# Halved selection for the first units, cheaper weight conversion and a new order of small steps in a top-k attention and MLP kernel

## The chip, the core and the metric

One core of a Trainium2 chip runs the whole program. Its engines are TensorE (matmuls and transposes), VectorE, ScalarE, GpSimd and SyncE, which issues the DMAs. In the profile they are PE (with PEld for its weight loads), DVE, ACT, POOL and SP. Every engine works through its own instructions strictly in their written order and waits on semaphores for the others. The metric is the device time of one execution in microseconds (us), smaller being better.

## What is computed

```python
scores = scale * np.matmul(q, k.transpose(0, 1, 3, 2))     # 8 batches, 8 heads, 576 x 576, head size 64
kth = np.partition(scores, -top_k, axis=-1)[..., -top_k:-top_k + 1]   # top_k = 32
scores = np.where(scores >= kth, scores, -1000000000.0)
attn = np.exp(scores - np.max(scores, axis=-1, keepdims=True))
attn = attn / (np.sum(attn, axis=-1, keepdims=True) + 1e-09)
x = np.matmul(attn, v)                                     # heads side by side: (8, 576, 512)
mu, var = x.mean(-1), x.var(-1)
xn = (x - mu) / np.sqrt(var + 1e-06) * g_ln
out = x + np.maximum(xn @ w_ch1, 0.0) @ w_ch2              # 512 -> 2048 -> 512
```

q, k, v and g_ln are float32. The two weights come as float64, as pairs of 32-bit words, and the kernel makes float32 of them itself.

## The kernel before

**Units.** The work is cut into units. A unit is one block of 128 query rows for both heads of a pair (two tiles of 128 x 576 scores), or, for the last 64 rows of a batch, a "rest" unit that packs both heads into one tile. Four head pairs and eight batches make 160 units. They are grouped into jobs of one batch, one head pair and some query blocks (L743 to 753): batch 0 has jobs with blocks [0, 1], then [2, 3], then the rest [4]; batch 1 has [0, 1] and [2, 3, 4]; all later ones [0, 1, 4] and [2, 3]. The units of a job form a group, whose attention is multiplied with v at once.

**Steps.** The main loop (L900 to 1023) runs one step n per unit and writes the instructions of all engines in a hand-made order. In step n, unit n is in selection on VectorE (`select`, in four parts 0 to 3), unit n + 1 gets its scores on TensorE (`scores`, evicted from PSUM by ScalarE, L335), unit n - 1 is masked on ScalarE (`mask`, `weigh`), and units n - 2 and n - 3 are transposed, multiplied with v (`values`) and scaled by the reciprocal of their sums (`place`). The first EARLY = 8 units are masked and turned one step sooner.

**Selection.** An unhalved unit takes the 8 largest of 576 values four times (L416) and overwrites them in between (L423). A halved unit first splits its scores into larger and smaller of each pair of columns k and k + 288 (`halve`, L363): hi by VectorE (L376), lo by GpSimd on the bits as integers, a + b - hi (L375, L377). It then merges the 16 largest of lo into hi (L390, L385) and selects from 304 columns (L398). Units 0 to 7 are unhalved, all others halved. `halve(n + 1)` stands in step n behind `select(n, 1)`.

**Weights.** 32 pieces of 128 x 512 weights are converted during steps -1 to 16. `split` takes three activations on ScalarE (L180, L181, L184) and a clamp on GpSimd (L185); a step later `shift` is one operation on VectorE (L188) and `join` two or three on GpSimd (L194, L198 for norm's factor in the first 16 pieces, L199). `batches` (L214) says how many pieces a step splits: four ahead of step 0, then 2 and 1 in turn up to step 7, then 2. The sign of a piece lies in one of four buffers, which its join frees.

**Blocks.** When two or three tiles of 128 rows of x are complete, they become a block for norm and MLP: VectorE takes its statistics (`stats`, L623), TensorE transposes x and multiplies (L667, L680, L697). Its matmuls wait in the list `todo`, from which `fill` puts a few into each gap of TensorE's order. `slot` (L864) sets how many: up to step 17 the estimated difference of VectorE's and TensorE's cost, later an even share that leaves 4 us of work when the next block arrives. The first block is given in step 9, and the group ahead of it is finished within step 8 (`quick`).

**Small steps.** `prepare` makes the bias of the exponential out of m's threshold and top, in two operations: on VectorE up to unit 16, on GpSimd later. From batch 2 on, `move` turns one head of most units by a VectorE transpose (L482) and five DMAs in place of TensorE. The reciprocals are at L932.

Of the kernel before, what the change touches and what calls it, by code (L numbers as in the profile page):

```python
# [10 lines left out]
ALU = mybir.AluOpType  # L11
# [5 lines left out]
TOP_K = 32  # L17
# [12 lines left out]
def kernel(  # L30
# [111 lines left out]
    class Piece:  # L142
# [26 lines left out]
        def split(self):  # L169
            def tmp(name, dt):  # L170
                return hpool.tile([P, DM], dt, tag="h", name=name)

            high = self.raw[:, :, 1].bitcast(FP32)
            self.size = tmp("size", U32)
            self.low = tmp("low", FP32)

            pl, tag = ((opool, "o"), (rpool, "r"))[self.i % 2]
            self.sign = pl.tile([P, DM], FP32, tag=tag, name="sign")
            size_f = self.size[:].bitcast(FP32)
            nc.scalar.activation(size_f, high, AF.Abs)  # L180
            nc.scalar.activation(  # L181
                self.low[:], self.raw[:, :, 0], AF.Copy, bias=2.0, scale=2.0**-51
            )
            nc.scalar.activation(self.sign[:], high, AF.Sign)  # L184
            nc.gpsimd.tensor_scalar(size_f, size_f, HIGH_MAX, HIGH_MIN, ALU.min, ALU.max)  # L185

        def shift(self):
# [4 lines left out]
        def join(self):  # L192
            size = self.size[:]
            nc.gpsimd.tensor_tensor(size, size, self.low[:].bitcast(U32), ALU.add)  # L194
            size = size.bitcast(FP32)
            if self.i < NF:
                gain = gcol[:, self.c : self.c + 1].to_broadcast([P, DM])
                nc.gpsimd.tensor_tensor(size, size, gain, ALU.mult)  # L198
            nc.gpsimd.tensor_tensor(self.dst, size, self.sign[:], ALU.mult)  # L199
            ready[self.i] = now[0]  # L200

# [13 lines left out]
    batches = {}  # L215
    queue = list(pieces)
    for n in range(-1, NF):
        count = 4 if n < 0 else 1 + (n + 1) % 2 if n < NF // 2 else 2
        batches[n], queue = queue[:count], queue[count:]
    assert not queue  # L220

# [86 lines left out]
    class Unit:  # L308
        def __init__(self, job, group, qt):
            self.job, self.group, self.qt = job, group, qt  # L310
            self.rest = qt == J
            self.tiles = [(0, 1)] if self.rest else [(0,), (1,)]

            self.moved = False

            self.halved = False
            self.e = None
            self.weighed = 0

# [43 lines left out]
    def halve(u):  # L363

        nt = len(u.tiles)  # L370
        u.lo = lopool.tile([P, 2, HALF], FP32, tag="lo", name="lo")
        u.hi = hipool.tile([P, 2, HALF + TOP_K // 2], FP32, tag="hi", name="hi")
        a, b = u.sc[:, 0:nt, 0:HALF], u.sc[:, 0:nt, HALF:S]
        lo, hi = u.lo[:, 0:nt], u.hi[:, 0:nt, 0:HALF]
        nc.gpsimd.tensor_tensor(lo.bitcast(I32), a.bitcast(I32), b.bitcast(I32), ALU.add)  # L375
        nc.vector.tensor_tensor(hi, a, b, ALU.max)  # L376
        nc.gpsimd.tensor_tensor(  # L377
            lo.bitcast(I32), lo.bitcast(I32), hi.bitcast(I32), ALU.subtract
        )

    def select_halved(u, i):
# [24 lines left out]
    def select(u, i):  # L406

        if u.halved:
            return select_halved(u, i)
        nt = range(len(u.tiles))  # L410
        if i == 0:
            u.cur = [u.sc[:, t] for t in nt]
            u.wk = {}
        m = small.tile([P, 2, 8], FP32, tag=f"m{i}", name=f"m{i}")
        for t in nt:
            nc.vector.max(m[:, t, :], u.cur[t])  # L416
        if i < TOP_K // 8 - 1:
            for t in nt:
                if i == 0:

                    o = (NF - 4 + 2 * t) * DM
                    u.wk[t] = w2[:].rearrange("p f n -> p (f n)")[:, o : o + S]
                nc.vector.match_replace(u.wk[t], m[:, t, :], u.cur[t], LOWEST)  # L423
                u.cur[t] = u.wk[t]
        if i == 0:
            u.top = m
        u.thr = m

    def prepare(u):

        nt = len(u.tiles)
        u.bias = small.tile([P, 2], FP32, tag="bias", name="bias")
        b = u.bias[:, 0:nt]

        engine = nc.vector if u.i < CONVERTING else nc.gpsimd
        engine.tensor_tensor(b, u.thr[:, 0:nt, 7], u.top[:, 0:nt, 0], ALU.subtract)  # L436
        engine.tensor_scalar(b, b, scale, 0.0, ALU.mult, ALU.add)  # L437

    def mask(u, t):
        if u.e is None:  # L440
# [306 lines left out]
    for b in range(B):  # L747
        parts = [[0, 1], [2, 3], [J]]
        if b:
            parts = [[0, 1], [2, 3]]  # L750
            parts[b < 2].append(J)
        for qts in parts:
            jobs += [Job(b, hp, [qts]) for hp in range(NHP)]
    units = []
# [18 lines left out]

    CONVERTING = max(n for n in batches if batches[n]) + 2
    EARLY = jobs[NHP].first
    for u in units[EARLY:]:
        u.halved = True

    for u in units[jobs[5 * NHP].first :]:
        u.moved = not u.rest and u is not u.group.units[-1]  # L780
# [12 lines left out]
    for j in jobs:  # L793
        if j.hp == NHP - 1:
            b = j.b
            step = j.last + (3 if j.last < EARLY else 4)
            tiles = [(b, qt) for g in j.groups for qt in g.qts if qt < J]
            dsts = [[(out[b, t[1] * P : (t[1] + 1) * P, :], full)] for t in tiles]
            if J in j.groups[0].qts and b % 2:

                step += 1
                tiles.append(("r", b // 2))
# [44 lines left out]
    def dve_cost(n):  # L847
        u, ex = at(n), after(n)[0]
        c = 5.0 if u is None else DVE_REST if u.rest else DVE_UNIT
        if u and u.halved:  # L850
            c *= DVE_HALVED
        return c + DVE_MOVE if ex and ex.moved else c

    def give(n):
# [39 lines left out]
    nc.sync.dma_start(grow[:], g_ln.rearrange("(c p) -> c p", p=P))  # L894
    load(fresh[1], nc.sync, nc.scalar)
    scores(units[0])
    load_gain()
    weights(-1, 0)
    weights(-1, 1)
    for n in range(END):  # L900
# [23 lines left out]
            values(g)  # L924
        if u:
            select(u, 0)
        if moved:
            move(ex)
        for store in sent:
            store()  # L930
        for den in recips.pop(n, []):
            nc.vector.reciprocal(den, den)  # L932
        if n == gives_first:
            for blk, i in rows_of.pop(n):
                blk.stats(i)
# [27 lines left out]
        if not quick:  # L963
            weights(n, 1)
        fill()
# [90 lines left out]
```

## Time and profile before

The time is 1665.68 us, the median of 3 runs (1665.18 to 1667.19). The profiled execution spans 1666.8 us:

| engine | busy us | share | instructions |
|---|---|---|---|
| TensorE | 1574.1 | 94% | 7113 |
| VectorE | 1464.5 | 88% | 4476 |
| ScalarE | 1077.2 | 65% | 2759 |
| GpSimd | 664.0 | 40% | 879 |

The largest groups of instructions: hidden matmuls L680, 550.0 us; output matmuls L697, 546.1; VectorE's L398, 460.7, and L385, 368.0; GpSimd's L375 and L377, 197.7 and 196.8; scores L354, 217.4, and their evictions L335, 199.2.

In the lines of the profile, L12 is line 12 of the kernel, "out<-in" names the tiles, "x4" counts instructions merged into one line, and what stands in square brackets is how long the engine was idle before and who ended that. Matmuls of float32 appear as two records each. An average over the span says little here, since the kernel has different limits at different times: it is read in stretches.

### The profile page before, as it was taken

How to read it: one execution, taken by the hardware profiler on the slowest of the kernel's cores; microseconds unless marked ns; L12 is line 12 of the kernel's file. 1: busy time of each engine (PE TensorE's matmuls, PEld its weight loads, DVE VectorE, ACT ScalarE, POOL GpSimd, SP SyncE). 2: the span in 40 equal slices, each digit the busy share in tenths (PEclk: the TensorE clock that was granted, in tenths of full speed). 3: DMA queues.
4: the chain of work that ended last, by engine and by line, in shares of the span. 5: the costliest groups of instructions: out<-in, count | busy, mean ns of one | idle time of the engine just before them, and what ended most of it. 6: DMA issues, size and time to landing. Idle time of an engine off the chain costs nothing.

```text
span 1666.8 us, 25284 instructions
## 1 busy us (share of the span) xinstructions
PE 1574.1 (94%) x7113; PEld 955.1 (57%) x7113; DVE 1464.5 (88%) x4476; ACT 1077.2 (65%) x2759; POOL 664.0 (40%) x879
## 2 busy tenths in 40 slices
PE   3568989989999999999999999999999999999998
PEld 1346556566555575755547575745547575755564
DVE  5998999999999999999999999899998999998000
ACT  5677967767666776767666675767666676665310
POOL 5567854343433434343343434343243433333010
PEclk9758999999999999999999999999999999999999
DMA  7423333001331133213231233112331132111000
GB/s 176 100 64 108 89 58 59 22 14 27 76 81 51 53 76 81 65 54 69 59 86 51 55 73 83 52 54 70 65 89 44 53 81 74 52 46 47 26 13 13
DMA packets 301203, 104.58 MB, mean 63 GB/s; under 512 B 246276, under 2 KB 283144, under 8 KB 301064
## 3 DMA queue, kind: packets, MB, share of 16 engines
q1 hardware_dynamic: 296328, 102.39, 24.4%
q10 hardware_dynamic: 4736, 0.59, 0.3%
q8 instruction: 57, 0.93, 0.2%
q14 instruction: 82, 0.67, 0.1%
HBM read 74.58 MB, written 28.31 MB: 62 GB/s over the span
## 4 chain that ended last, share of the span: by engine, by line
PE 71%; DVE 21%; issue 4%; ACT 2%; POOL 1%; DMA 1%; ACTq 0%; POOLq 0%; DVEq 0%; SPq 0%
PE hps L680 25%; PE ops L697 24%; PE scps L354 8%; PE av L563 6%; DVE m L398 5%; DVE hi L385 4%; PE tp L505 4%; DVE hi L390 2%; DVE m L416 2%; PE av L570 2%; DVE w L423 2%; DVE lo L385 1%; DVE hi L376 1%; DVE size L188 1%; PE tp L667 1%
## 5 line engine op out<-in xcount | busy, mean ns | idle before, releaser
L680 PE MATMUL hps<-xT,w 128*128 128x256 f32 (+1 forms) x2048 | 550.0, 411 | 2.7 <-ACT xT L672 2.3
L697 PE MATMUL ops<-w,h 128*128 128x512 f32 x1152 | 546.1, 599 | 0.0
L398 DVE MAX8 m<-hi 128x8 f32<-128x304 f32 x1088 | 460.7, 458 | 2.3
L680 PEld LDWEIGHTS hps<-xT,w 128*128 128x128 f32 x2048 | 372.1, 191 | 108.5 <-issue 17.3
L385 DVE MATCH_REPLACE8 hi<-m,hi 128x304 f32<-128x304 f32 x816 | 368.0, 456 | 0.0
L375 POOL TENSOR_TENSOR lo<-sc 128x576 int32<-128x576 int32 (+1 forms) x152 | 197.7, 1301 | 316.3 <-ACT sc L335 156.9
L697 PEld LDWEIGHTS ops<-w,h 128*128 128x128 f32 x1152 | 200.2, 191 | 169.9 <-issue 164.6
L377 POOL TENSOR_TENSOR lo<-lo,hi 128x576 int32<-128x576 int32 (+1 forms) x152 | 196.8, 1295 | 141.9 <-DVE hi L376 139.7
L354 PE MATMUL scps<-kT,qT 64*128 64x288 f32 (+3 forms) x1344 | 217.4, 433 | 32.4 <-DVE qT L304 20.9
L335 ACT COPY sc<-scps 128x288 f32<-128x288 f32 x576 | 199.2, 409 | 62.3 <-PE scps L354 51.0
L442 ACT ACTIVATE e<-sc,m 128x576 f32<-128x576 f32 x288 | 224.3, 779 | 9.7 <-DVE m L398 6.2
L452 ACT ACTIVATE e<-e,bias 128x576 f32<-128x576 f32 x288 | 224.6, 780 | 2.9 <-DVE bias L437 2.5
L390 DVE MAX8 hi<-lo 128x8 f32<-128x288 f32 x544 | 221.8, 443 | 2.6 <-POOL lo L377 1.5
L354 PEld LDWEIGHTS scps<-kT,qT 64*128 64x128 f32 (+1 forms) x1344 | 122.4, 181 | 146.6 <-issue 56.2
L505 PEld LDWEIGHTS tp<-ident,e 128*128 128x128 f32 x864 | 110.9, 147 | 115.9 <-ACT e L452 51.7
L505 PE MATMUL tp<-ident,e 128*128 128x128 f32 x864 | 138.1, 285 | 38.2 <-ACT e L452 37.9
L692 ACT ACTIVATE h<-hps 128x256 f32<-128x256 f32 (+1 forms) x256 | 105.9, 414 | 96.5 <-PE hps L680 93.8
L436 POOL TENSOR_TENSOR bias<-m,m 128x2 f32<-128x2 f32 (+1 forms) x143 | 27.8, 195 | 303.6 <-DVE m L398 303.6
L563 PE MATMUL av<-pt,vb 128*64 128x256 f32 (+2 forms) x1088 | 146.7, 413 | 0.0
L376 DVE TENSOR_TENSOR hi<-sc 128x576 f32<-128x576 f32 (+1 forms) x152 | 138.8, 913 | 5.5 <-ACT sc L335 5.5
L385 DVE MATCH_REPLACE8 lo<-hi,lo 128x288 f32<-128x288 f32 x272 | 118.2, 440 | 0.0
L517 ACT COPY pt<-tp 128x512 f32<-128x512 f32 x128 | 74.6, 583 | 62.1 <-PE tp L505 60.5
(79 smaller groups left out, 1295.0 us busy)
## 6 DMA issues: line engine op xcount, KB each, us to landing
turned<-sc SPq DMA_DIRECT2D x72, 256.0 KB, 2.0
pt<-turned SPq DMA_DIRECT2D x288, 64.0 KB, 2.0
vb<-in_v_dram SPq DMA_DIRECT2D x136, 128.0 KB, 2.5
raw<-in_moe_w_ch_dram SPq DMA_DIRECT2D x32, 512.0 KB, 4.0
kin<-in_k_dram SPq DMA_DIRECT2D x128, 72.0 KB, 2.5
qin<-in_q_dram SPq DMA_DIRECT2D x120, 72.0 KB, 2.5
out_dram<-o SPq DMA_DIRECT2D x32, 256.0 KB, 2.2
ends<-in_v_dram SPq DMA_DIRECT2D x136, 16.0 KB, 2.2
```

Source lines behind the costliest of these rows:

```text
L335: nc.scalar.copy(u.sc[:, t, s * HALF : (s + 1) * HALF], made[s][t][:, 0:HALF])
L354: nc.tensor.matmul(ps[i * R : i * R + ql, o : o + width], qT[r, q0 : q0 + ql], kT[r, k0 : k0 + width], start=True, stop=True,)
L375: nc.gpsimd.tensor_tensor(lo.bitcast(I32), a.bitcast(I32), b.bitcast(I32), ALU.add)
L385: nc.vector.match_replace(x[:, t], m[:, t, :], x[:, t], LOWEST)
L390: nc.vector.max(u.hi[:, t, o : o + 8], u.lo[:, t])
L398: nc.vector.max(m[:, t, :], u.hi[:, t])
L442: nc.scalar.activation(u.e[:, t], u.sc[:, t], AF.Prelu, bias=u.thr[:, t, 7:8], scale=-1.0, alpha=SLOPE)
L452: nc.scalar.activation(u.e[:, t], u.e[:, t], AF.Exp, bias=u.bias[:, t : t + 1], scale=-scale / SLOPE, accum_out=g.den[:, col : col + 1],)
L505: nc.tensor.transpose(ps[:, c * P : (c + 1) * P], u.e[:, t, c * P + t * R : (c + 1) * P + t * R], ident[:],)
L563: nc.tensor.matmul(av[h * D : (h + 1) * D, 0 : g.nq], vb[:, h * J + c, :], g.ptB[:, 0 : g.nq // 32, c, :] if h else g.pt[:, c, 0 : g.nq], ...
L680: nc.tensor.matmul(ps["h"][:, 0:N], w1[:, c, f * P : (f + 1) * P], xT[0][:, c, 0:N], start=(c == 0), stop=(c == NC - 1),)
L697: nc.tensor.matmul(ps[i][:], hT[f][:, i * P : (i + 1) * P], w2[:, f, :], start=(f == 0), stop=(f == NF - 1),)
```

## The change

It has six parts. (1) The first eight units are halved too, with both hi and lo by VectorE; for the others, GpSimd's two operations now both come behind VectorE's, as a - hi + b. (2) Norm's factor is multiplied into the sign by ScalarE in `split`, no longer by GpSimd in `join`. (3) Steps 0 to 7 split two pieces each, and steps 8 to 15 two and one in turn. (4) A bias on VectorE is one operation per tile, with the top as scalar operand, instead of two per unit. (5) Within a step, `move` and the reciprocals come behind the halving and the turn of new heads, and `stats` behind `select(u, 2)` (not in the first block's step). (6) In the last batch the rest units come first, as jobs of their own, and the last two tiles of batch 6 wait to form one block with the rest tile. They are for relieving GpSimd and VectorE at the beginning, for fewer waits in VectorE's order, and for smaller blocks at the end.

```diff
             nc.scalar.activation(self.sign[:], high, AF.Sign)
+            if self.i < NF:
+                nc.scalar.mul(self.sign[:], self.sign[:], gcol[:, self.c : self.c + 1])
             nc.gpsimd.tensor_scalar(size_f, size_f, HIGH_MAX, HIGH_MIN, ALU.min, ALU.max)
...
             size = size.bitcast(FP32)
-            if self.i < NF:
-                gain = gcol[:, self.c : self.c + 1].to_broadcast([P, DM])
-                nc.gpsimd.tensor_tensor(size, size, gain, ALU.mult)
             nc.gpsimd.tensor_tensor(self.dst, size, self.sign[:], ALU.mult)
...
-        count = 4 if n < 0 else 1 + (n + 1) % 2 if n < NF // 2 else 2
+        count = 4 if n < 0 else 2 if n < NF // 2 else 1 + (n + 1) % 2
...
-        nc.gpsimd.tensor_tensor(lo.bitcast(I32), a.bitcast(I32), b.bitcast(I32), ALU.add)
         nc.vector.tensor_tensor(hi, a, b, ALU.max)
+        if u.i < EARLY:
+
+            nc.vector.tensor_tensor(lo, a, b, ALU.min)
+            return
         nc.gpsimd.tensor_tensor(
-            lo.bitcast(I32), lo.bitcast(I32), hi.bitcast(I32), ALU.subtract
+            lo.bitcast(I32), a.bitcast(I32), hi.bitcast(I32), ALU.subtract
         )
+        nc.gpsimd.tensor_tensor(lo.bitcast(I32), lo.bitcast(I32), b.bitcast(I32), ALU.add)
...
-        engine = nc.vector if u.i < CONVERTING else nc.gpsimd
-        engine.tensor_tensor(b, u.thr[:, 0:nt, 7], u.top[:, 0:nt, 0], ALU.subtract)
-        engine.tensor_scalar(b, b, scale, 0.0, ALU.mult, ALU.add)
+        if u.i < CONVERTING:
+
+            for t in range(nt):
+                nc.vector.tensor_scalar(
+                    b[:, t : t + 1], u.thr[:, t, 7:8], u.top[:, t, 0:1], scale,
+                    ALU.subtract, ALU.mult,
+                )
+            return
+        nc.gpsimd.tensor_tensor(b, u.thr[:, 0:nt, 7], u.top[:, 0:nt, 0], ALU.subtract)
+        nc.gpsimd.tensor_scalar(b, b, scale, 0.0, ALU.mult, ALU.add)
...
             parts = [[0, 1], [2, 3]]
-            parts[b < 2].append(J)
+            if b < B - 1:
+                parts[b < 2].append(J)
+            else:
+                parts = [[J]] + parts
...
+            if b == B - 2 and units[-1].job.b == B - 1 and J - 1 in j.groups[0].qts:
+
+                kept = (tiles, dsts)
+                continue
             if J in j.groups[0].qts and b % 2:
+                if not tiles:
+                    tiles, dsts = kept
...
     scores(units[0])
+    halve(units[0])
     load_gain()
...
         if u:
             select(u, 0)
-        if moved:
-            move(ex)
         for store in sent:
             store()
-        for den in recips.pop(n, []):
-            nc.vector.reciprocal(den, den)
...
             select(u, 1)
-        if nxt and nxt.halved:
+        if nxt:
             halve(nxt)
         if n in turns:
             turn_heads(turns[n])
...
-        for blk, i in rows_of.pop(n, []):
-            blk.stats(i)
+        for den in recips.pop(n, []):
+            nc.vector.reciprocal(den, den)
+        if moved:
+            move(ex)
         if not quick:
             weights(n, 1)
...
             select(u, 2)
+        for blk, i in rows_of.pop(n, []):
+            blk.stats(i)
```

More of the change, by code (lines that the diff above doesn't have):

```diff
@@ L314, in __init__ @@
             self.moved = False
-            self.halved = False
             self.e = None
@@ L374, in halve, with select @@
         lo, hi = u.lo[:, 0:nt], u.hi[:, 0:nt, 0:HALF]
-        nc.gpsimd.tensor_tensor(lo.bitcast(I32), a.bitcast(I32), b.bitcast(I32), ALU.add)
         nc.vector.tensor_tensor(hi, a, b, ALU.max)
+        if u.i < EARLY:
+            nc.vector.tensor_tensor(lo, a, b, ALU.min)
+            return
         nc.gpsimd.tensor_tensor(
-            lo.bitcast(I32), lo.bitcast(I32), hi.bitcast(I32), ALU.subtract
+            lo.bitcast(I32), a.bitcast(I32), hi.bitcast(I32), ALU.subtract
         )
-    def select_halved(u, i):
+        nc.gpsimd.tensor_tensor(lo.bitcast(I32), lo.bitcast(I32), b.bitcast(I32), ALU.add)
+    def select(u, i):
         nt = range(len(u.tiles))
@@ L404, in select_halved @@
             u.thr = m
[L406 to L427, printed above, removed]
     def prepare(u):
@@ L775 @@
     EARLY = jobs[NHP].first
-    for u in units[EARLY:]:
-        u.halved = True
     for u in units[jobs[5 * NHP].first :]:
@@ L849, in dve_cost @@
         c = 5.0 if u is None else DVE_REST if u.rest else DVE_UNIT
-        if u and u.halved:
-            c *= DVE_HALVED
+        c *= DVE_HALVED
         return c + DVE_MOVE if ex and ex.moved else c
```

## The prediction

> **What bounds the kernel now.** I read first where each engine is busy, in stretches of 50 us (columns: stretch, then busy us and instruction count for each engine, granted TensorE clock, DMA share, GB/s).
>
> ```profile
> core 0: us, PE busy (x) PEld busy (x) DVE busy (x) ACT busy (x) POOL busy (x), PEclk, DMA share, GB/s
> 0.00:50.00 50.00, 15.83 (x51) 9.13 (x51) 32.37 (x66) 28.61 (x61) 27.32 (x35) 1.00 0.64 147
> 50.00:100.00 50.00, 30.33 (x118) 17.94 (x120) 49.73 (x109) 38.17 (x91) 27.73 (x27) 0.66 0.47 114
> 100.00:150.00 50.00, 37.24 (x155) 26.57 (x154) 45.14 (x121) 31.82 (x76) 32.46 (x29) 0.73 0.22 67
> 150.00:200.00 50.00, 48.50 (x234) 30.23 (x233) 49.66 (x153) 48.24 (x117) 44.18 (x39) 1.00 0.42 117
> 550.00:600.00 50.00, 50.00 (x252) 32.00 (x250) 50.00 (x162) 36.34 (x94) 21.52 (x27) 1.00 0.28 68
> 1600.00:1650.00 50.00, 50.00 (x187) 34.52 (x186) 0.00 (x0) 8.77 (x20) 3.16 (x4) 1.00 0.03 6
> ```
>
> TensorE is full from about 450 us to 1661.8, where its last matmul ends, and VectorE is the full one in the first 150. A busy TensorE need not run at its peak, so I compared every run of equal matmuls (say eight records of L680) with the fastest tenth of its kind: from 450 to 1500 the excess is about 1 us in 50. So after 450 the time is a fixed amount of TensorE work, and nothing that VectorE, ScalarE or GpSimd saves there counts. The excess, gaps included, is 29 us in 150 to 350 and 7 in 350 to 450. What can move the end is (1) when the first block's hidden matmuls start, at 132.3 now, (2) these 36 us, (3) TensorE work added or removed.
>
> Next, what holds TensorE in 150 to 450 (waiter, releaser, total us, times, longest):
>
> ```profile
> PE tp L667 <- POOL x L638: 5.3, 2, 4.8
> PE scps L354 <- DVE qT L304: 4.2, 2, 3.3
> PE tp L505 <- ACT e L452: 3.2, 3, 1.8
> PE scps L354 <- ACT x L579: 2.5, 2, 1.8
> ```
>
> VectorE or its followers end all of these. Third, ScalarE from unit 1's masks to unit 8's (31 to 112 us), its busy time and waits:
>
> ```profile
> 31.00:112.00 81.00, 46.25 (x179) 27.97 (x179) 74.04 (x159) 60.63 (x141) 48.97 (x46) 0.74 0.38 97
> ```
>
> ```profile
> ACT oT L575 <- PE av L570: 9.1, 3, 3.9
> ACT sc L335 <- PE scps L354: 5.3, 8, 1.1
> ```
>
> Of 81.0 us it works 60.6 and waits 14.4 for TensorE. Last, VectorE in order of time:
>
> ```profile
> 38.92 0.82 DVE L188 TENSOR_SCALAR size<-size 128x512 uint32<-128x512 uint32 x1 [6.55 <-POOL size L185]
> ...
> 137.36 1.00 DVE L436 TENSOR_TENSOR bias<-m,m 128x2 f32<-128x2 f32 x1
> ...
> 147.62 2.40 DVE L188 TENSOR_SCALAR size<-size 128x512 uint32<-128x512 uint32 x2
> ```
>
> It waits 6.55 us once for GpSimd's joins. A bias of two columns takes 1.00 and two shifts 2.40 where free ones take 0.16 and 0.75: they wait out a running GpSimd instruction.
>
> **The skill.** The Trainium skill, GPSIMD Engine Reference, section 8 (Key points), says that GpSimd shares its SBUF interfaces with VectorE and contends with instructions of two SBUF inputs or in a 2-port mode. The trace agrees: L376 takes 0.74 us (median of 80) with GpSimd idle at its start and 1.23 (mean of 72) with it busy. VectorE: DVE Perf Modes, The perf-mode tier table, gives fp32 tensor_scalar twice tensor_tensor's rate; here L188 advances 512 columns in 0.335 us and L376 576 in 0.676. Perfetto Trace Analysis, Identifying the Most-Contended Engine, warns that matmul busy share doesn't measure distance from the peak; hence the comparison above.
>
> **Part 1, halves for the first eight units.** Unhalved, a unit costs VectorE 8 x 0.668 (L416) + 6 x (0.065 + 0.659) (L423) = 9.69 us. On halves: max and min 2 x 0.676, 4 x 0.360 (L390), 2 x 0.427, 8 x 0.377 (L398), 6 x 0.443 = 9.3. It saves 0.4 a unit, if min costs what max does and finds GpSimd idle; a GpSimd instruction in the way would add up to 1.3. But unit 1's halving is now queued in step 0 and waits for its scores, whose evictions stand on ScalarE behind the first four pieces (20.93 us now).
>
> **Part 2, norm's factor.** GpSimd loses 16 x 1.04 us (L198). ScalarE gains 16 multiplications. An independent 512-column activation starts 0.56 us after the one before; one that reads its predecessor's result must wait for it to end (L184 takes 0.66), so a piece grows from 1.69 to 2.38.
>
> **Part 3, two pieces a step.** Steps 1, 3, 5, 7 get one more piece each (1.69 on ScalarE), steps 9, 11, 13, 15 one less.
>
> **Parts 1 to 3 together, up to the first block.** ScalarE's first four pieces end 4 x 0.69 = 2.8 later, so unit 1's scores are there at about 25.0, VectorE having finished select(0, 1) at 17.4: a wait of 7.6 us takes the place of the 6.55. Behind it are turn, shifts and the rest of unit 0, and behind the shifts GpSimd's joins, which free the sign buffers. ScalarE's step 1 starts at 34.7 instead of 31.5 (+3.2). From there to step 8 it gets 4 x 1.69 + 10 x 0.69 = 13.7 us more. Its slack is 81.0 - 60.6 - 12.2 = 8.2, because the waits for av (9.1) and most of those for scores recur: av comes behind scores on TensorE, and those wait for ScalarE to free PSUM. So step 8 starts 3.2 + 13.7 - 8.2 = 8.7 us later. Step by step I get 8.3 (119.6 for 111.3): an odd step of 14.5 us, an even one of 11.0, against 23.3 for two now. ScalarE replaces VectorE as the bound there. The chain from step 8 to the first hidden matmul (quick values, x, two pieces, scores, xT) has 1.1 us of idle ScalarE to lose, so the hidden start moves from 132.3 to **139.5: +7.2 us**. It could be +4, if the multiplication overlapped like the rest (0.13 x 16 = 2 us) and scores came sooner, or +9.
>
> **Part 4, from there to unit 17.** VectorE reaches unit 11 4.4 us late (its bias and shifts save 2.8). Units 11 to 15 took 53.7: 43.0 of selection and halving, 4.6 of shifts, 5.5 of biases, 0.6 of rest. Now there are 8 shifts instead of 10, right behind the max and before GpSimd can start its subtraction: 2.7. Whether a one-column tensor_scalar waits for GpSimd no row shows: at least 0.35 each, at most the 1.1 of now, 1.8 to 5.5 for five. With 0.9 of other contention, 48.4 to 52. Unit 16 saves 1 to 2. So unit 17 starts between 3 us earlier and 1 later: I take 1 earlier. TensorE allows it: behind the later start it can recover 3.5 us of its own excess by unit 16 and is still ahead of VectorE, so most of the 6.6 us that it waits at 208 to 218 go.
>
> **Part 5, the order of later steps.** With both GpSimd operations behind the max, L376 no longer waits: 1.2 us between units 17 and 22, 0.4 at 330. At 336.5 TensorE waits 4.8 us for x: statistics move behind select(u, 2), and GpSimd has two operations of 1.4 before it: +1.3. Reciprocals move some 2.3 to 3.7 us back, and ScalarE's scaling of x waits for them with its evictions behind it (1.4, 2.0 and 1.2 us at 296 to 330 now). Scores there are a step ahead of VectorE, which hides it. Moves cost nothing: values that read them come two steps later. After 350 VectorE saves another 2.5 us (L376), which may shorten the 4.8 us that TensorE loses at 444 to 448, where a mask waits for VectorE's m; I count 2.
>
> **Part 6, the last batch's order.** The rest tiles get groups of their own: av costs 2.41 + 0.89 instead of 2.95, four times: +1.4. The second unit of each pair is now last in its group, so TensorE turns its second head instead of a DMA: 4 x 0.44 = +1.8. The same blocks are computed, and TensorE has no gap there to close.
>
> **Sum:** -1 (unit 17) - 1.2 - 0.4 + 1.3 - 2 + 3.2 = -0.1, so **1665.6 us**, no change.
>
> **Rivals.** *Faster:* the early delay is small. If the hidden start moves by 2 only, unit 17 comes some 6 us earlier, and the rest sums to about -8: 1658. For it: 36 us of excess are there to be had, and 20 us of ScalarE's 81 are idle. Against it: 14 of these are waits that recur. *Slower:* the delay stays. If the one-column bias and min wait for GpSimd as now, and ScalarE's later scaling holds TensorE, only about 3 of the 7.2 come back; with +1.3 and +3.2 that is +8: 1673. For it: TensorE is at its peak from 132 to 205 but for 3.5 us, and can't catch up more. Against it: VectorE's waits at 137 to 218 are real and have fewer causes left. A third, that k and q loads for four one-unit jobs in a row arrive late, adds 1 to 3 us at the end and belongs to the slower side; 8 issues take 4 us and land 2.5 later, inside a step of 9.
>
> **Numbers.** Forecast 0.40, faster 0.33, slower 0.27. The range 1656 to 1674 takes in both rivals. The forecast spreads over the bound of 3.3 us on either side, so faster by over 0.2% gets 0.38, within 0.30, slower 0.32.
>
> **What would show it.** A wait of VectorE of 7 to 8 us for sc at about 17; ScalarE's evictions for unit 9 at about 119 instead of 111; the first hidden matmul near 139; L436 gone, and its tensor_scalar near 0.2 or near 1.0; L376 near 0.74 throughout; TensorE's excess in 150 to 450 well under 36. A hidden start before 134, or ScalarE still idle at 50 to 100, would prove the central step wrong.

## The result, and the profile after

The changed kernel takes 1679.47 us (median of 4 runs, 1678.92 to 1683.84); the kernel before takes 1665.54 beside it (4 runs, 1665.18 to 1667.19). The ratio is 1.0087, with a 95% interval of 1.0069 to 1.0106: 14 us slower, where the prediction said 1665.6, no change, and 1674 at most. The profiled execution spans 1682.0 us against 1666.8; it is the slowest of the four, some 4 us above the others, so single microseconds below are taken from several traces.

First, where each engine is busy, in the stretches shown of before:

```profile
core 0: us, PE busy (x) PEld busy (x) DVE busy (x) ACT busy (x) POOL busy (x), PEclk, DMA share, GB/s
0.00:50.00 50.00, 15.03 (x49) 8.20 (x50) 33.17 (x92) 33.85 (x68) 22.42 (x29) 1.00 0.67 168
50.00:100.00 50.00, 31.86 (x102) 16.99 (x101) 42.59 (x141) 39.47 (x86) 24.95 (x24) 0.93 0.45 106
100.00:150.00 50.00, 34.01 (x123) 20.72 (x121) 43.30 (x131) 33.84 (x79) 31.43 (x27) 0.63 0.31 90
150.00:200.00 50.00, 49.28 (x244) 34.80 (x243) 45.70 (x151) 42.28 (x103) 35.60 (x32) 0.97 0.20 59
550.00:600.00 50.00, 50.00 (x230) 29.34 (x229) 49.93 (x166) 36.08 (x89) 21.76 (x31) 1.00 0.28 67
1600.00:1650.00 50.00, 50.00 (x204) 35.16 (x203) 1.64 (x4) 10.93 (x27) 5.16 (x8) 1.00 0.03 11
```

VectorE is no longer full between 50 and 100 (42.6 of 50 us, against 49.7). In the two stretches shown after 550 TensorE is as full as before, so most of the loss lies ahead of them or is more work. The first hidden matmul, in order of time on TensorE, starts at 143.46 us instead of 132.30:

```profile
143.46 8.92 PE L665 MATMUL hps<-xT,w 128*128 128x256 f32 x31 [2.98 <-ACT xT L657]
```

ScalarE from unit 1's masks to unit 8's is now the stretch 35 to 124, 89 us instead of 81. Its busy time, and then what it waits for:

```profile
35.00:124.00 89.00, 56.53 (x179) 30.26 (x179) 75.53 (x251) 73.01 (x161) 47.30 (x45) 0.84 0.40 104
```

```profile
ACT oT L560 <- PE av L555: 12.3, 3, 4.4
ACT sc L332 <- PE scps L351: 2.8, 7, 0.5
```

ScalarE works 73.0 of 89 us and waits 15.1 for TensorE. Its waits for VectorE have gone, which in the kernel before (31 to 112 us) were:

```profile
ACT e L442 <- DVE m L416: 2.7, 1, 2.7
ACT e L452 <- DVE bias L437: 2.5, 3, 0.9
```

So ScalarE is the bound here. Next, VectorE in order of time:

```profile
23.72 0.76 DVE L372 TENSOR_TENSOR hi<-sc 128x576 f32<-128x576 f32 x1 [6.38 <-ACT sc L332]
26.84 3.52 DVE L190 TENSOR_SCALAR size<-size 128x512 uint32<-128x512 uint32 x4
...
133.80 0.33 DVE L416 TENSOR_SCALAR bias<-m,m 128x1 f32<-128x1 f32 x2
```

The wait for unit 1's scores is there, 6.4 us at 17.3. A unit's bias, two operations now, takes 0.33 us. Last, what holds TensorE between 150 and 450, and between 400 and 800 (waiter, releaser, total us, times, longest):

```profile
PE tp L652 <- POOL x L623: 4.6, 1, 4.6
PE tp L490 <- ACT e L437: 3.4, 3, 1.8
PE scps L351 <- DVE den L950: 2.3, 1, 2.3
PE scps L351 <- DVE qT L303: 0.8, 1, 0.8
```

```profile
PE av L548 <- DMA vb<-in_v_dram: 2.4, 2, 1.8
PE scps L351 <- ACT xT L657: 0.9, 1, 0.9
```

Two waits are new: for the reciprocals `den`, and for the DMA that brings v.

**An account of TensorE's time.** As in the prediction, each run of equal matmuls is compared with the fastest tenth of its kind, here over all 18 traces. From the first hidden matmul on, that makes a sum: the start, the excess over the fastest (gaps included), the work at its fastest, and 5 us after the last matmul.

| kernel | hidden start | excess to 350 us | 350 to 800 | after 800 | work | span |
|---|---|---|---|---|---|---|
| before | 132.3 | 30.6 | 14.8 | 16.0 | 1468.1 | 1666.8 |
| changed | 143.5 | 25.5 | 19.7 | 16.8 | 1471.4 | 1682.0 |
| difference | +11.2 | -5.1 | +4.9 | +0.8 | +3.3 | +15.2 |
| predicted | +7.2 | -8.5 | -2 | 0 | +3.2 | -0.1 |

(Predicted, to 350: 8.2 recovered up to unit 17, 1.2 and 0.4 less of L376, 1.3 more for late statistics.) The experiments take these columns one after another.

### The profile page after: what moved, and what is told of

Same layout as the page of the kernel before. It is cut to its first block, busy times and chain, and to the rows that moved or that the text cites. A ratio compares the mean times of both kernels' runs of the same rounds, so it can differ in the third digit from the quotient of the medians.

```text
span 1682.0 us, 25369 instructions
## 1 busy us (share of the span) xinstructions
PE 1589.8 (95%) x7201; PEld 962.7 (57%) x7201; DVE 1423.7 (85%) x4551; ACT 1092.0 (65%) x2783; POOL 644.7 (38%) x863
## 4 chain that ended last, share of the span: by engine, by line
PE 56%; issue 3%; ACT 1%; DMA 0%; DVE 0%; POOL 0%; SPq 0%; POOLq 0%; ACTq 0%
PE hps L665 19%; PE ops L682 19%; PE scps L351 6%; PE av L548 5%; PE tp L490 3%; PE av L555 2%; PE tp L652 1%; PE xo L587 0%; PE tp L523 0%; DMA turned<-sc 0%; POOL o L695 0%; DMA vb<-in_v_dram 0%; ACT sc L332 0%; ACT xT L657 0%; ACT e L427 0%
## 5 line engine op out<-in xcount | busy, mean ns | idle before, releaser
L400 DVE MAX8 m<-hi 128x8 f32<-128x304 f32 x1152 | 487.9, 460 | 3.3
L377 POOL TENSOR_TENSOR lo<-sc,hi 128x576 int32<-128x576 int32 (+1 forms) x152 | 195.9, 1289 | 554.1 <-DVE hi L372 331.1
L387 DVE MATCH_REPLACE8 hi<-m,hi 128x304 f32<-128x304 f32 x864 | 390.1, 457 | 0.0
L351 PE MATMUL scps<-kT,qT 64*128 64x288 f32 (+3 forms) x1344 | 224.0, 433 | 41.5 <-DVE qT L303 21.8
L392 DVE MAX8 hi<-lo 128x8 f32<-128x288 f32 x576 | 235.3, 445 | 16.9 <-POOL lo L380 15.7
L372 DVE TENSOR_TENSOR hi<-sc 128x576 f32<-128x576 f32 (+1 forms) x160 | 113.3, 708 | 118.2 <-ACT sc L332 117.9
L380 POOL TENSOR_TENSOR lo<-lo,sc 128x576 int32<-128x576 int32 (+1 forms) x152 | 194.8, 1281 | 11.9
L548 PE MATMUL av<-pt,vb 128*64 128x256 f32 (+2 forms) x1152 | 152.8, 404 | 2.5 <-DMA vb<-in_v_dram 2.4
L387 DVE MATCH_REPLACE8 lo<-hi,lo 128x288 f32<-128x288 f32 x288 | 125.3, 441 | 0.0
L548 PEld LDWEIGHTS av<-pt,vb 128*64 128x64 f32 x1152 | 78.6, 142 | 70.3 <-issue 29.3
```

The lines of the kernel that those rows point to most:

```text
L351: nc.tensor.matmul(ps[i * R : i * R + ql, o : o + width], qT[r, q0 : q0 + ql], kT[r, k0 : k0 + width], start=True, stop=True,)
L377: nc.gpsimd.tensor_tensor(lo.bitcast(I32), a.bitcast(I32), hi.bitcast(I32), ALU.subtract)
L548: nc.tensor.matmul(av[h * D : (h + 1) * D, 0 : g.nq], vb[:, h * J + c, :], g.ptB[:, 0 : g.nq // 32, c, :] if h else g.pt[:, c, 0 : g.nq], ...
```

## Experiments

"Changed" below is the changed kernel; a time's ratio is always to the kernel before, measured beside it. Four of the experiments (undo_gain, undo_pieces, undo_order and undo_last) were to part three theories: A, ScalarE's load before the first block; B, the last batch's order; C, the new places of move, reciprocals and stats.

**ScalarE's load.** Part 2 or part 3 undone, then both, and both alone on the kernel before. The edits, in the order pieces, factor:

```diff
-        count = 4 if n < 0 else 2 if n < NF // 2 else 1 + (n + 1) % 2
+        count = 4 if n < 0 else 1 + (n + 1) % 2 if n < NF // 2 else 2
...
-            if self.i < NF:
-                nc.scalar.mul(self.sign[:], self.sign[:], gcol[:, self.c : self.c + 1])
...
+            if self.i < NF:
+                gain = gcol[:, self.c : self.c + 1].to_broadcast([P, DM])
+                nc.gpsimd.tensor_tensor(size, size, gain, ALU.mult)
```

> The changed kernel (1679.5 us) with part 2 undone: norm's factor is again multiplied in by GpSimd, not by ScalarE. Theory A (ScalarE is overloaded up to the first block, and the late start of the hidden matmuls, 143.5 us against 132.3, is carried to the end one for one): ScalarE has 14 x 0.7 = 9.8 us less before step 8, of which its step time follows about half, so the hidden start falls to about 138 and the time to about 1674. Theory B (the early delay is hidden later, and the last batch's order costs the time): under 2 us less, 1678. Theory C (the new places of move, reciprocals and stats eat what the later steps could win back): under 2 us less, 1678.

> The changed kernel with part 3 undone: steps 0 to 7 split two and one piece in turn, steps 8 to 15 two. Theory A: ScalarE has 4 x 2.4 = 9.6 us less before step 8, so the hidden start falls to about 137 and the time to about 1673, if the four pieces that now fall in steps 9 to 15 don't hold TensorE there. Theory B: under 2 us less. Theory C: under 2 us less.

> The changed kernel with parts 2 and 3 undone: norm's factor on GpSimd, and two and one pieces in turn up to step 7. Theory A: ScalarE has its old load, steps 1 to 8 take 23.5 us for two again or less, the hidden start falls from about 142 to 131 or 132, and the time by 10 to 11 us to about 1669. If the start and the end aren't tied one for one (undoing part 3 alone brought the start 7 us forward and the end only 3), the time falls by 6 us only, to 1673.

> The kernel before with parts 2 and 3 alone: norm's factor on ScalarE and two pieces in each of steps 0 to 7. Theory A: the hidden start goes from 131 (three traces: 130.1 to 132.3) to about 142, and the end follows as far as TensorE has no stall left to absorb it: by 5 to 7 us, 1671 to 1674, since undoing both in the changed kernel gave back 6.5. If the end follows in full: 1677. If VectorE's late biases and halves had hidden it: under 1668.

| kernel | ratio (95%) | hidden start | excess to 350 | 350 to 800 |
|---|---|---|---|---|
| changed | 1.0087 (1.0069 to 1.0106) | 143.5 | 25.5 | 19.7 |
| undo_gain | 1.0057 (1.0040 to 1.0074) | 137.8 | 25.7 | 20.1 |
| undo_pieces | 1.0068 (1.0053 to 1.0083) | 135.8 | 26.7 | 19.0 |
| undo_gain_pieces | 1.0048 (1.0034 to 1.0061) | 130.1 | 27.8 | 19.9 |
| gain_pieces_alone | 1.0026 (1.0017 to 1.0036) | 139.9 | 25.4 | 14.6 |

The multiplication and the doubled pieces bring the late start: either is worth some 5 to 8 us of it, both about 12 in the changed kernel. Theory A holds in its first half. The end doesn't follow one for one: of the 12 us that undoing both brings forward, 0.39% of the time, 6.5 us, comes out at the end, and on the kernel before the two add 4.4 us, not 8.6. TensorE's excess is smaller behind a later start (25.4 against 30.6 up to 350). VectorE is less far behind: in gain_pieces_alone it starts unit 17 3.8 us later (219.8 against 216.0, the mean of four traces of the old order), where the hidden start is 8.6 later, so its results are ready sooner after TensorE wants them. The intervals of undo_gain and undo_pieces overlap both that of changed and that of undo_gain_pieces, so the times don't settle what either does alone.

Why was the start so late? Here is ScalarE in order of time between the last pt copy and the copy of oT, in a step with two pieces of the kernel before and then of the changed one:

```profile
74.81 0.29 ACT L539 COPY pt<-tp 128x128 f32<-128x128 f32 x1
76.19 0.40 ACT L335 COPY sc<-scps 128x288 f32<-128x288 f32 x1 [1.09 <-PE scps L354]
77.15 1.00 ACT L335 COPY sc<-scps 128x288 f32<-128x288 f32 x3 [0.56 <-PE scps L354]
80.94 0.37 ACT L575 COPY oT<-av 128x256 f32<-128x256 f32 x1 [2.79 <-PE av L570]
```

```profile
82.93 0.27 ACT L524 COPY pt<-tp 128x128 f32<-128x128 f32 x1
83.08 1.01 ACT L332 COPY sc<-scps 128x288 f32<-128x288 f32 x3
84.44 0.40 ACT L332 COPY sc<-scps 128x288 f32<-128x288 f32 x1 [0.34 <-PE scps L351]
89.20 0.37 ACT L560 COPY oT<-av 128x256 f32<-128x256 f32 x1 [4.36 <-PE av L555]
```

From the last pt to oT it is 6.13 us before and 6.27 after: av needs the last pt, and ScalarE needs av. What it no longer waits for scores it waits for av: 4.44 us of waits in this stretch became 4.70. None of this took up the added work.

**The order within a step.** All of part 5 undone, then the place of `move` alone undone; then, on the kernel before, move late; move late but with the k and q loads behind it; and move late with v's loads ahead of the k and q loads and of move. The edit of undo_move, from behind the loads to behind select(u, 0); late_move is the same the other way:

```diff
+        if moved:
+            move(ex)
...
         if n in turns:
             turn_heads(turns[n])
...
                 load(fresh[later], nc.sync, nc.sync)
...
-        if moved:
-            move(ex)
```

> The changed kernel with part 5 undone: move and the reciprocals directly behind select(u, 0), stats ahead of the weights, as before. Theory C: the stalls of TensorE at 281 (2.5 us), 341 (4.7) and 451 to 456 (6.7) shrink or go, and the time falls by 5 us or more, to 1674. Theories A and B: within 2 us of 1679.5; the stall at 341 shrinks by 1.3 us at most.

> The changed kernel with one piece of part 5 undone: move stands directly behind select(u, 0) again, ahead of the turn of new heads and the eight k and q loads; reciprocals and stats stay where the change put them. Theory D (the move's six DMAs now stand on SyncE's queue behind the eight loads of a step with a turn, and the loads of v behind them, so av waits for v at 456 and 675 us): the waits for vb go, TensorE's excess in 400 to 800 falls from 15 us to about 10, and the time falls by 4 to 6 us, to about 1674, as with all of part 5 undone. Theory C' (reciprocals or stats are what costs): no change, 1679.

> The kernel before with one edit: move stands behind the turn of new heads and the loads of k and q, as in the changed kernel. Theory D: v lands late in the steps with a turn, the excess in 400 to 800 rises by 4 to 5 us, and the time from 1665.7 to about 1670. Theory C': no change, 1665.7. The prediction counted nothing for this edit.

The loads put behind move, as an edit of late_move:

```diff
         if n in turns:
             turn_heads(turns[n])
-            later = fresh.index(turns[n]) + 1
-            if later < len(fresh):
-                load(fresh[later], nc.sync, nc.sync)
         if moved:
             move(ex)
+        if n in turns:
+            later = fresh.index(turns[n]) + 1
+            if later < len(fresh):
+                load(fresh[later], nc.sync, nc.sync)
```

> The kernel before, with move behind the turn of new heads as in late_move (1.0029 of before), but with the loads of k and q put behind move, so that SyncE issues the move's transfers ahead of them. On VectorE the order is that of late_move. Theory D (it is the order on SyncE's queue that costs): as before, 1665.7, excess in 400 to 800 at 10. If move's place on VectorE is what costs: as late_move, 1670.5.

Then, from late_move again, v's loads taken from the end of the step to ahead of the turn of new heads:

```diff
+        if n > EARLY and mk and mk is units[mk.job.last]:
+            load_values(mk.job)
         if n in turns:
             turn_heads(turns[n])
...
-        for x in (u if n < EARLY else None, mk if n > EARLY else None):
-            if x and x is units[x.job.last]:
-                load_values(x.job)
+        if n < EARLY and u and u is units[u.job.last]:
+            load_values(u.job)
```

> The kernel of late_move (1.0029 of before; move behind the turn of new heads and the k and q loads) with the loads of v issued ahead of all of these in their step. Theory D' (v lands late because its loads are last on SyncE's queue, behind a move that becomes ready later): no wait for vb, excess in 400 to 800 back at 10, 1665.7 as before. If move's place on VectorE costs: 1670.5.

| kernel | ratio (95%) | hidden start | excess to 350 | 350 to 800 |
|---|---|---|---|---|
| undo_order | 1.0044 (1.0029 to 1.0059) | 141.2 | 21.7 | 14.9 |
| undo_move | 1.0052 (1.0039 to 1.0065) | 142.0 | 22.2 | 17.3 |
| late_move | 1.0029 (1.0019 to 1.0040) | 131.1 | 30.6 | 19.5 |
| move_then_load | 1.0056 (1.0044 to 1.0069) | 130.1 | 30.5 | 21.7 |
| late_move_early_v | 0.9996 (0.9988 to 1.0004) | 131.8 | 30.5 | 14.7 |

Moving one VectorE operation and its five DMA issues makes the kernel before 0.29% slower, 4.8 us, nearly all of it as excess between 350 and 800 (3.1 us at 430 to 455 us, 0.5 at 639 and 1.2 at 667, the last two within av). SyncE's DMA issues of a step with a turn of new heads show how. Before, and then changed:

```profile
436.49 0.34 SPq L487 DMA_DIRECT2D turned<-sc  x1
438.51 1.75 SPq L489 DMA_DIRECT2D pt<-turned  x4
440.36 2.00 SPq L278 DMA_DIRECT2D kin<-in_k_dram  x4
442.47 2.17 SPq L278 DMA_DIRECT2D qin<-in_q_dram  x4
444.69 0.49 SPq L290 DMA_DIRECT2D vb<-in_v_dram  x1
```

```profile
444.84 1.94 SPq L277 DMA_DIRECT2D kin<-in_k_dram  x4
446.88 2.06 SPq L277 DMA_DIRECT2D qin<-in_q_dram  x4
449.04 0.44 SPq L472 DMA_DIRECT2D turned<-sc  x1
451.61 1.90 SPq L474 DMA_DIRECT2D pt<-turned  x4
453.56 0.43 SPq L289 DMA_DIRECT2D vb<-in_v_dram  x1
```

SyncE issues in order and waits in between: L474 comes only when L472's transfer has landed, 2.0 to 2.6 us after its issue. In the changed kernel, from 400 to 800 us, SyncE's own waits for this are:

```profile
SPq L474 <- DMA turned<-sc: 43.4, 22, 3.9
```

(The Trainium skill, DMA: Bandwidth & Descriptors, Rules for kernel authors, asks for exactly this wait where one DMA reads what another wrote; this is its price for all that stands behind.) v stands last: it is issued 8.7 us after the first k load instead of 4.3, and in the changed kernel av waits for it:

```profile
456.08 5.58 PE L548 MATMUL av<-pt,vb 128*64 128x320 f32 x16 [1.78 <-DMA vb<-in_v_dram]
```

My first explanation, that the eight loads ahead of move are the harm, fell with move_then_load: with move ahead of them it got slower still (1.0056 against 1.0029). The trace shows the wait that grew there:

```profile
PE av L563 <- DMA vb<-in_v_dram: 4.5, 2, 3.0
```

What counts is how long v stands behind a move that becomes ready late. In late_move the k and q issues at least fill the time until move is ready; in move_then_load they, and v behind them, wait for move and its landing (k is issued at 442.07 instead of 438.27 us). late_move_early_v decides that v is what is late: move is as late on VectorE and its issue as late as in late_move (443.06 against 442.47 us), only v goes first,

```profile
436.05 0.43 SPq L290 DMA_DIRECT2D vb<-in_v_dram  x1
...
443.06 0.43 SPq L487 DMA_DIRECT2D turned<-sc  x1
```

and the loss is gone. (In late_move the waits list names ScalarE's score copies for 1.6 us of av's wait and v's DMA for 0.5 only. Where several semaphores are waited for, one name is shown; the edit, not that name, is the evidence. Another wait that late_move brings, 1.8 us for `e` from ScalarE at about 435 us, stays at 1.3 with early v, and yet the excess from 430 to 455 is 4.6 us there against 4.8 of before; so it isn't the loss.)

Undo_move is not all of part 5: its excess from 350 to 800 is 17.3 against 14.9 with the whole order undone. From halves_bias_old_order below, stats alone were put late:

```diff
-        for blk, i in rows_of.pop(n, []):
-            blk.stats(i)
         if not quick:
             weights(n, 1)
...
             select(u, 2)
+        for blk, i in rows_of.pop(n, []):
+            blk.stats(i)
```

> The kernel of halves_bias_old_order with stats alone behind select(u, 2), as in the changed kernel. If stats make the wait of 2.3 us for the rest tile at 450: as halves_bias, 1665.5. If the reciprocals do: as halves_bias_old_order, 1662 to 1664.

It takes 0.9990 (0.9981 to 0.9998) against 0.9971 (0.9959 to 0.9982) with stats early: 3 us, though the two intervals just touch. In the two profiles 2.4 us of it show as excess. On TensorE, in order of time, this wait is new:

```profile
450.14 0.66 PE L653 MATMUL tp<-ident,r 128*128 128x128 f32 x4 [1.95 <-POOL r L624]
```

It counts for 0.7 us of the excess only (15.6 against 14.9 from 350 to 800), because TensorE waits less just ahead of it. The other 1.6 us lie before 350, nearly all at 338 us, where the same eight matmuls take longer behind a wait that both kernels have. In late_stats, and then in halves_bias_old_order:

```profile
338.62 5.76 PE L683 MATMUL ops<-w,h 128*128 128x512 f32 x8
```

```profile
336.18 4.22 PE L683 MATMUL ops<-w,h 128*128 128x512 f32 x8
```

These eight take 4.2 to 5.8 us in the other traces too, with early stats as with late ones (5.48 in pool_order_alone, with early ones). So the times show that late stats cost something, and the wait at 450 shows one place; how much of the 3 us belongs to it stays open.

With the reciprocals late as well (halves_bias) it is 0.9993: the reciprocals cost nothing that these runs can tell.

**The last batch's order.** Part 6 undone:

```diff
-            if b < B - 1:
-                parts[b < 2].append(J)
-            else:
-                parts = [[J]] + parts
+            parts[b < 2].append(J)
...
-            if b == B - 2 and units[-1].job.b == B - 1 and J - 1 in j.groups[0].qts:
-
-                kept = (tiles, dsts)
-                continue
             if J in j.groups[0].qts and b % 2:
-                if not tiles:
-                    tiles, dsts = kept
```

> The changed kernel with part 6 undone: the last batch's rest units are back in the first jobs, the last blocks are as before. Theory B (the order of the last batch costs what the unit times seem to show, 8 us): 1671.5. Theory A and C: it costs what the prediction counted, 4 x 0.35 of av and 4 x 0.44 of transposes: 1676.3.

The ratio is 1.0051 (1.0036 to 1.0066), 6 us below changed, but both intervals together leave 2 to 10. The account is sharper: the work is 1468.1 instead of 1471.4, and the excess after 800 is 16.1 against 16.8. By it the order costs 3.3 us of added matmuls and under 1 us of gaps, so theory B falls.

**Halves and biases.** From the changed kernel, parts 2, 3, 6 and the late move undone (halves_bias), then all of part 5 too; from the kernel before, part 4 with GpSimd's new order (bias_alone), and each of these two edits by itself (bias_only the upper one, pool_order_alone the lower one):

```diff
-        engine = nc.vector if u.i < CONVERTING else nc.gpsimd
-        engine.tensor_tensor(b, u.thr[:, 0:nt, 7], u.top[:, 0:nt, 0], ALU.subtract)
-        engine.tensor_scalar(b, b, scale, 0.0, ALU.mult, ALU.add)
+        if u.i < CONVERTING:
+
+            for t in range(nt):
+                nc.vector.tensor_scalar(
+                    b[:, t : t + 1], u.thr[:, t, 7:8], u.top[:, t, 0:1], scale,
+                    ALU.subtract, ALU.mult,
+                )
+            return
+        nc.gpsimd.tensor_tensor(b, u.thr[:, 0:nt, 7], u.top[:, 0:nt, 0], ALU.subtract)
+        nc.gpsimd.tensor_scalar(b, b, scale, 0.0, ALU.mult, ALU.add)
...
-        nc.gpsimd.tensor_tensor(lo.bitcast(I32), a.bitcast(I32), b.bitcast(I32), ALU.add)
         nc.vector.tensor_tensor(hi, a, b, ALU.max)
         nc.gpsimd.tensor_tensor(
-            lo.bitcast(I32), lo.bitcast(I32), hi.bitcast(I32), ALU.subtract
+            lo.bitcast(I32), a.bitcast(I32), hi.bitcast(I32), ALU.subtract
         )
+        nc.gpsimd.tensor_tensor(lo.bitcast(I32), lo.bitcast(I32), b.bitcast(I32), ALU.add)
```

> The changed kernel with parts 2, 3 and 6 and the place of move undone: what is left is halves for units 0 to 7, one-operation biases, both GpSimd operations behind the max, and reciprocals and stats in their new places. By the account of TensorE (hidden start 131.5, excess 5 to 9 us less than the 61.7 of before, as in the changed kernel with part 5 undone, and the work of before, 1467.8): 1656 to 1660, faster than both kernels. If the late hidden start was what let VectorE get ahead (so that the excess comes back with the early start): 1664 to 1666.

> The changed kernel with parts 2, 3, 5 and 6 undone: halves for units 0 to 7, one-operation biases and both GpSimd operations behind the max remain. From halves_bias (0.9993 of before, TensorE's account: start 131.5, excess 59.8): the wait of 2.3 us for the rest tile's norm at 450 goes with the reciprocals and stats in their old places, so some 2 us less: 1662 to 1664. If those places don't matter: 1665.5.

> The kernel before with part 4 and the order of GpSimd's two operations alone; units 0 to 7 are unhalved. It parts what the halves do from what the biases do. By the prediction's steps the halves save VectorE 0.4 us a unit, 3 us by the first block's step, and ScalarE and VectorE are close to each other there, so the hidden start is 132 to 133 against 131.5 with halves, and the time 1 us above halves_bias_old_order: 1663 to 1665. If the one-operation biases bring nothing, it is 1665.7.

> The kernel before with one edit: both of GpSimd's operations of a halving stand behind VectorE's max. The prediction counted 1.6 us of waits of L376 for this. If it is what makes bias_alone faster: 1661. If the biases are: the hidden start stays at 130 to 132 and the time at 1664 to 1666.

> The kernel before with the one-operation biases alone (GpSimd's operations in their old order). Seventeen biases took VectorE 11.8 + 3.2 = 15.0 us in before and take 5.5 in bias_alone. If VectorE's time in steps 0 to 16 passes to the end, and the parts add (bias_alone 0.9962, GpSimd's order alone 1.0016): 9 us faster than before, 1657.5. If they don't add, because the biases' gain is what GpSimd's order let through: as bias_alone, 1660.5, or slower.

| kernel | ratio (95%) | hidden start | excess to 350 | 350 to 800 |
|---|---|---|---|---|
| halves_bias | 0.9993 (0.9984 to 1.0001) | 131.5 | 27.9 | 15.7 |
| halves_bias_old_order | 0.9971 (0.9959 to 0.9982) | 129.4 | 25.8 | 14.9 |
| bias_alone | 0.9962 (0.9948 to 0.9975) | 127.0 | 25.9 | 14.9 |
| pool_order_alone | 1.0016 (1.0010 to 1.0023) | 131.3 | 33.5 | 15.1 |
| bias_only | 0.9972 (0.9961 to 0.9983) | 127.6 | 28.1 | 14.7 |

halves_bias missed its first expectation: its excess is only 1.8 us below that of before, not 5 to 9, and it isn't clearly faster. bias_alone missed too, to the other side: its hidden start is 127.0, not 132 to 133. At 1660.6 us it has the lowest time of all, 6 us below the kernel before, but can't be told from halves_bias_old_order and bias_only. What the three share are the biases. VectorE's groups for them, before (two lines) and in bias_only (name, shapes, count, then busy us and mean ns):

```profile
L436 DVE TENSOR_TENSOR bias<-m,m 128x2 f32<-128x2 f32 (+1 forms) x17 | 11.8, 697 | 0.6
L437 DVE TENSOR_SCALAR bias<-bias 128x2 f32<-128x2 f32 (+1 forms) x17 | 3.2, 191 | 0.6
```

```profile
L438 DVE TENSOR_SCALAR bias<-m,m 128x1 f32<-128x1 f32 x33 | 5.5, 204 | 0.0
```

15.0 us become 5.5. Nine of the 17 units come ahead of the first block, where VectorE is the full engine, and the hidden start comes 4 us earlier: 127.3, the mean of the two kernels with the new biases and unhalved first units, against 131.3, the mean of the four traces that are the kernel before up to there (132.3, 131.1, 130.1, 131.8).

Halving the first units costs: the start is 127.0 without and 130.7 with it (mean of 129.4, 131.5, 131.8 and 130.1). A halved unit is 0.34 us shorter on VectorE (10.29 for 10.63, units 3 and 5), but the halving queued in step 0 waits for scores, and unit 2 starts at 45.9 us instead of 43.0. The times of the two, 0.9971 and 0.9962, can't be told apart.

GpSimd's new order alone is slower, which neither theory had expected, and with the biases it does nothing that can be told (0.9962 against 0.9972). With it TensorE waits 6.3 or 6.4 us for x from GpSimd at about 325 to 342, instead of 4.8, as long as the reciprocals stay early; with late ones (halves_bias, changed) it waits 4.6. Which of GpSimd's operations is in the way, and why the biases should undo that, wasn't tried and stays open.

## Why the prediction was wrong

- **The bound and the three things that move the end.** Right. From hidden start, excess and work each span is accounted for; after 800 no kernel's excess lies more than 1.3 us from that of before.
- **The wait for unit 1's scores, and step 1.** Right: 6.4 us at 17.3 (7.6 predicted), and ScalarE's first mask comes 2.7 us later (35.35 for 32.62; 3.2 predicted). A piece with its multiplication takes 2.45 us (2.38 predicted).
- **"Its slack is 81.0 - 60.6 - 12.2 = 8.2."** This is the first step that failed, in the size of one term. It took 12.2 of ScalarE's 14.4 us of waits for TensorE as fixed, and let the rest absorb work. All of them stay (15.1 now); only the 5.2 us that ScalarE spent waiting for VectorE's m and biases went. So the slack was 5.2 us and not 8.2. From first mask to step 8 it is 13.7 - 5.2 = 8.5 longer, measured 9.0 (35.35 to 124.84 against 32.62 to 113.13), and not 5.5; its evictions for unit 9 start at 123.1, not 119.6. The hidden start moved by 11.2 in the two profiles, 11.3 in the means of four and of three traces (142.6 against 131.3), instead of 7.2. It even lies outside the range of 4 to 9 given for it.
- **Parts 1 and 4 ahead of the first block.** Nothing was counted for biases there, since ScalarE was to be the bound, and 0.4 a unit for halves. By themselves the biases are worth -4.0 us of the start and the halves +3.7, which nearly cancel. That the halving's wait takes the place of another one was right for the changed kernel, with ScalarE so late, but wrong as a saving.
- **Part 4, up to unit 17.** The way was right: VectorE makes up 8.8 of 11.3 us (unit 17 starts at 218.5, mean of three traces, against 216.0, mean of four), where 8.2 were counted. Between units 11 and 17 it is 5.5 us faster, and 5.4 were counted. As the delay had been put 4 us too small, unit 17 is 2.5 late instead of 1 early. The one-column operation, 0.35 to 1.1 us in the bounds, takes 0.20.
- **Excess to 350.** 8.5 less was predicted; 5.1 less came in the profile. In undo_last and undo_move, which have the same instructions up to there, it is 22.1 and 22.2, some 8.5 less. The 3 us between are the clock, below. The sum was right, in part by luck: the 1.3 us more that late statistics were to cost at 336 did not come (TensorE waits 4.6 us there, 4.8 before).
- **"Moves cost nothing: values that read them come two steps later."** This is the second step that failed, and the larger one. The reader of the moved data does have time; what stands behind the move on SyncE's queue has not. It was -2 at 444 to 448 and is +4.9 from 350 to 800, 6.9 us off, where the start is 4.0 off. late_move alone costs 4.8 us, late stats up to 3. With all of part 5 undone the excess there is 14.9, as before, so the gain of 2 didn't come either. The third rival named loads that arrive late, but k's and q's in the last batch, not v's.
- **Part 5, L376.** Its mean fell from 913 to 708 ns (L372), but GpSimd's order alone did not make the kernel faster.
- **Part 6.** Right: +3.2 predicted, +3.3 in the account.
- **The rivals.** The slower one was nearest, 1673, but for another reason: it had the delay stay, and the delay was recovered as far as the forecast said. It was larger from the start, and no rival had moves that hold up v, or TensorE waiting for the rest tile behind late statistics.

Worked out from single edits, the parts add up to 0.68%: parts 2 and 3 +0.26 (alone), move +0.29 (alone), stats +0.19 and reciprocals +0.03 (on halves_bias_old_order), halves +0.09 and biases with GpSimd's order -0.38, part 6 +0.20 (3.3 us). Measured is 0.87 (0.69 to 1.06). The sum is rough, since most of these edits were timed in other kernels than the changed one: there TensorE doesn't wait for r at 462 us at all, because v has already made av late. From the other end, undoing parts 2 and 3 gives back 0.39, part 5 0.43 and part 6 0.36. So no part alone is the cause; parts 2 and 3 and part 5 are the two large ones, and only the biases help.

## What to carry to other kernels

An engine's waits are slack only if what they wait for doesn't itself wait for that engine: follow the releaser back one round, as from the pt copy to oT here, before you let added work vanish in them. When a DMA is moved within an in-order issue queue, list what stands behind it, not only who reads it; a pair of DMAs that must land in between holds up the whole queue, and what is needed next should be issued ahead of it. Undo and add each part by itself: here one edit of six was worth keeping.

## What the runs showed of the hardware

A VectorE operation with one column and a scalar operand never waited for GpSimd: in bias_only all 33 start while a GpSimd instruction runs, and take 188 to 215 ns. Of the two-column operations with two inputs in the kernel before, 16 of 17 start beside a running GpSimd instruction and take 271 to 1130 ns; the other one takes 161. The Trainium skill, SBUF — State Buffer, section "SBUF: two separate sides", says that VectorE and GpSimd lock each other out whole instructions long where VectorE has two SBUF inputs or a 2-port mode. The trace agrees for two inputs. Whether it is the one column or the scalar in place of a second tensor that keeps the new operation free of it, no run here parts.

TensorE ran at about half rate for some microseconds after a short wait in one execution, and not in another that has the same instructions up to there. Four records of the same matmul, in both cases after a wait of 0.7 us, in the changed kernel and in undo_last:

```profile
183.45 1.63 PE L351 MATMUL scps<-kT,qT 64*128 64x288 f32 x6 [0.72 <-ACT x L564]
185.01 2.08 PE L665 MATMUL hps<-xT,w 128*128 128x256 f32 x4
```

```profile
182.10 1.63 PE L351 MATMUL scps<-kT,qT 64*128 64x288 f32 x6 [0.71 <-ACT x L564]
183.66 1.13 PE L665 MATMUL hps<-xT,w 128*128 128x256 f32 x4
```

The granted clock of the stretch 180 to 190 is 0.83 in the first and 1.00 in the second, and so again at 220 to 230. That is the 3 us by which the two excesses up to 350 differ.
